# Last eight gate/up chunks on 64-row halves, two numerators moved among them, and a last tile pair that takes one tile at a time

## The chip, the cores and the metric

The kernel runs on one core of a Trainium2 chip. It is written instruction by instruction for the core's engines: TensorE (PE) for matmuls, VectorE (DVE) and ScalarE (ACT) for elementwise work and for reading PSUM, GpSimd (POOL), and SyncE (SP), whose queue starts most DMAs. PSUM, where matmuls put their results, has eight banks of 512 float32 columns in 128 partitions. The metric is device time in microseconds (us) for the whole program.

## The reference

There are 2048 tokens (x is 2048 x 640), two branches on the same x, and a gate per token that mixes them:

```python
qkv = x @ wqkv                      # 32 heads of 20
pq, pk = q @ w_phi, k @ w_phi       # per head
phi_q = concat(softmax(pq), softmax(-pq));  phi_k likewise
kv, z = sum_s phi_k * v,  sum_s phi_k
a = ((phi_q @ kv) / (phi_q @ z + 1e-6)) @ wo          # linear attention
b = (gelu(x @ w_gate) * (x @ w_up)) @ w_down          # F = 1728
g = sigmoid((x * gate_w).sum(-1))
out = g * a + (1 - g) * b
```

All inputs and the output are bfloat16.

## The kernel before, in words

Tokens are cut into 16 tiles of 128 and four blocks of four tiles. F is cut into 13 chunks of 128 columns and a tail of 64 (chunk 13). D = 640 is five pieces of 128 (`KD`). A first stage (up to some 81 us) loads x and the weights, computes q, k, v, the exponentials of the features, and sums the attention state `KV`. The change lies in what follows, `ffn`, which issues three kinds of work in a fixed order. Every engine runs its own instructions in program order; `_Sched.op` adds a semaphore wait where an instruction reads or overwrites what another engine writes or still reads (a bank of PSUM is one unit, `("ps", bank)`).

**Gate/up** (`gateup`, matmuls recorded at L464). For a block of 512 tokens and a chunk, five matmuls of 128 rows and 512 columns put x @ w_gate into one bank and five put x @ w_up into another. ScalarE writes Gelu of the first (L779), VectorE multiplies by the second into `hT` (L781). The tail chunk does gate and up in one bank; there VectorE multiplies twice (L792), one time for each half of 64 partitions, and only for every other tile, since the two halves serve tiles of different parity. Chunks take two pairs of banks in turn, (0,1) and (6,7). Each block's chunks run in the order 0, 1, 13, 2, ..., 12.

**Numerators** (`num`, `num_mms` L817, `num_steps`). For one tile, 22 matmuls of 64 rows and 66 columns (phi_q times the state, for the two signs of the softmax in alternation) fill parts of four banks, 2 to 5. VectorE then divides: eight short steps of 32 columns (L851 to L858, the first of them a reciprocal), two multiplies of 640 columns that read PSUM (`O`, L863), and one add (`Og`, L866). A DMA on SP's queue transposes Og into `goT`. The four banks come free when the second multiply at L863 has ended, since each of the two is recorded as a reader of all four. In the kernel before, tiles 0 and 1 are done together in block 1 (`num_pair`): 44 matmuls behind the fifth chunk, into six banks, with the division's steps spread over the chunks that follow, which meanwhile use other banks. The other tiles are done in the down stage.

**Down** (`down_pair`, matmuls L898). Two tiles are done together, b @ w_down and a @ wo summed in one bank for each tile and column part. All matmuls have 64 rows: the two halves of the array work at the same time, one on the first and one on the second tile, on the upper or lower 64 rows of each piece. In an opening pass each half does its rows for its tile; in a closing pass the halves change tiles. A wait on a key `("turn", bank)` keeps the two halves from writing one bank at the same time. Output columns are cut in two parts of 320, and in the last pair in parts of 256, 256 and 128, so that the last part is short. `evac` scales by the gate into `outsb` (ScalarE, and in the last pair VectorE for the second tile) and SP's queue writes the output.

A generator yields after each pair of matmuls; `downs` counts these pairs (148 in a block: 2 x (38 opening + 36 closing)) and calls `num` after certain counts. Before, these are 1, 31, 61 and 91 in blocks 0 to 2, for tiles 4b + 2 to 4b + 5, and 1 and 31 in block 3:

```python
at = (1, 31, 61, 91)
...
for b in range(self.NB):
    downs(b, {at[k]: 4 * b + 2 + k for k in range(4 if b < 3 else 2)})
```

Block 3's `hT` has no room of its own; it takes the space of x for tiles 0 to 11, which is read for the last time in block 2.

Of the kernel before, what the change touches and what calls it, by code (L numbers as in the profile page):

```python
# [3 lines left out]
P = 128  # L4
BF16 = mybir.dt.bfloat16
F32 = mybir.dt.float32
AF = mybir.ActivationFunctionType
ALU = mybir.AluOpType
# [99 lines left out]
class _Kernel:  # L108
    S, D, H, DH, F = 2048, 640, 32, 20, 1728
    KD = D // P  # L110
# [4 lines left out]
    NFC = 14  # L115
    FR = F - 13 * P
    DA = DH + 1
    DB = DH + 2
# [641 lines left out]
    def gateup(self, b, c, banks):  # L760
# [7 lines left out]
        if c < 13:  # L768
# [5 lines left out]
            for w, wk, bk in ((self.wg_sb, "wg", banks[0]), (self.wu_sb, "wu", banks[1]))[:1 if done else 2]:  # L774
                for kt in range(self.KD):
                    key = self.upheld(c)[1] if early and wk == "wu" else (wk, i, kt)
                    self.mm(bk, 0, 512, w[:, kt, c * P:(c + 1) * P], xs(kt), kt == 0, kt == self.KD - 1, xr + [key])
            up, upk = (self.upheld(c)[0], ("upf", c)) if done else (self.bank(banks[1]), ("ps", banks[1]))
            sc.op("act", lambda e: e.activation(self.gl[:, slot, :], self.bank(banks[0]), AF.Gelu_apprx_tanh),  # L779
                  reads=[("ps", banks[0])], writes=[("gl", slot)], guard=self.oldw)  # L780
            sc.op("dve", lambda e: e.tensor_tensor(hT, up, self.gl[:, slot, :], ALU.mult),  # L781
                  reads=[upk, ("gl", slot)], writes=[("hT", hk, c)], guard=old)
        else:
# [6 lines left out]
            for r in (0, 1):  # L790
                odd = lambda v: v.rearrange("p (u r q) -> p u r q", r=2, q=P)[:, :, r, :]
                sc.op("dve", lambda e: e.tensor_tensor(  # L792
                    odd(hT[64 * r:64 * r + 64, :]), odd(self.ps[64:128, bk * 512:bk * 512 + 512]),
                    odd(self.gl[64:128, slot, :]), ALU.mult),
                    reads=[("ps", bk), ("gl", slot)], writes=[("hT", hk, c, r)], guard=old)

    def before_num(self):
        return ([("upf", c) for c in self.UP + self.LATE] + ["kstage", "qstage"] + [("wref", k, h) for k in (0, 3) for h in (0, self.HM)] + [("wref", k, 0) for k in (1, 2, 4)] + [("xtok", k) for k in range(4)] + ["wkT", "wqT"])

    def num(self, t):  # L800
        NBK, DB, old = self.NUMB, self.DB, self.before_num()
        w = self.HG * DB
        base = [(NBK + 2 * s) * 512 + 512 - 6 * w for s in (0, 1)]
        self.num_mms(t, base, 0)
        rb = [("ps", NBK + k) for k in range(4)]
        for step in self.num_steps(t, base, rb, old):
            step()

    def num_mms(self, t, base, late):
        sc, w = self.sc, self.HG * self.DB  # L810
        for g in range(self.G):
            n = min(w, self.H * self.DB - w * g)
            for s in (0, 1):
                a, o = 64 * s, base[s] + w * g
                edge = o // 512 != (o + w) // 512
                first = g == 0 or (o - w) // 512 != o // 512
                sc.op("pe", lambda e: e.matmul(  # L817
                    self.ps[:, o:o + n], self.Eq[a:a + 64, g, t * P:(t + 1) * P], self.KV[a:a + 64, g, 0:n],
                    start=first and not (late and g == 0), stop=edge or g == self.G - 1, skip_group_check=True),
                    reads=[("Eq", t), "KVd", ("KV", 0), ("KV", 8), ("KV", 10)], writes=[("ps", o // 512)],  # L820
                    signal=edge or g == self.G - 1)

    def num_pair(self):
        w = self.HG * self.DB
        top = 512 - 6 * w
        over = 512 + 512 - 3 * w
        bases = [[(2 + 3 * s) * 512 + c for s in (0, 1)] for c in (top, over)]
        rb = [("ps", b) for b in range(2, 8)]
        steps = []
        for t in (0, 1):  # L830
            self.num_mms(t, bases[t], t)
        for t in (0, 1):
            n = {0: (0, 1, 3, 4), 1: (1, 2, 4, 5)}[t]
            steps.append(self.num_steps(t, bases[t], [rb[k] for k in n], self.before_num()))
        return steps

    def num_steps(self, t, base, rb, old):
# [7 lines left out]
        key = lambda k: ("RH", sl, k)  # L845
        small, wide, fin = [], [], []
        into = small

        def dve(fn, reads, writes, guard=()):
            into.append(lambda: sc.op("dve", fn, reads=reads, writes=writes, guard=guard))  # L850
        dve(lambda e: e.reciprocal(R(0), Dn[1]), rb, [key(0)], guard=old)  # L851
# [6 lines left out]
        dve(lambda e: e.tensor_tensor(R(7), R(6), R(1), ALU.mult), [key(6), key(1)], [key(7)])  # L858
        into = wide
        for s, dst in ((0, self.O1), (1, self.O2)):  # L860
# [3 lines left out]
                rb + [key(6 + s)], [("O", s, sl)], guard=old)  # L864
        into = fin
        dve(lambda e: e.tensor_tensor(self.Og[:, sl, :], self.O1[:, sl, :], self.O2[:, sl, :], ALU.add),  # L866
            [("O", 0, sl), ("O", 1, sl)], [("Og", sl)], guard=old)
        gs = t % 8
        fin.append(lambda: sc.dma("sp", lambda e: e.dma_start_transpose(self.goT[:, gs, :, :], self.Og[:, sl, :]),
                                  reads=[("Og", sl)], writes=[("goT", gs)], guard=old))  # L870

        def run(part):
            for f in part:
                f()
        return [lambda p=p: run(p) for p in (small, wide, fin)]

    def down_pair(self, t0, banks, widths):

        sc = self.sc
        ts = (t0, t0 + 1)  # L880
        NFC, KD = self.NFC - 1, self.KD
        nw = len(widths)
        hk = t0 // 4
        last = t0 + 2 == self.NT
        os_ = t0 % 4

        def mm(r, j, h, c, opens, x, n):
            t = ts[j]
            tt, gs, bk, w0, a = t % 4, t % 8, banks[h][j], sum(widths[:h]), 64 * r
            w, end = widths[h], x == n - 1  # L890
            if c <= NFC:
# [11 lines left out]
        def evac(h):  # L903
            w0, w = sum(widths[:h]), widths[h]
            for j in (0, 1):
                bk, dst, g = banks[h][j], self.outsb[:, os_ + j, w0:w0 + w], self.Gm[:, ts[j]:ts[j] + 1]
                rd, wr = [("ps", bk), "Gm"], [("outsb", os_ + j, h)]
                if last and j == 1:
                    sc.op("dve", lambda e: e.tensor_scalar(dst, self.bank(bk, w), g, None, op0=ALU.mult), reads=rd, writes=wr)
                else:  # L910
                    sc.op("act", lambda e: e.activation(dst, self.bank(bk, w), AF.Copy, scale=g), reads=rd, writes=wr)  # L911
            if last:
                hs, c0, c1 = [h], w0, w0 + w
            elif h == nw - 1:
                hs, c0, c1 = range(nw), 0, self.D
            else:
                return
            if t0 < self.TB:
                rows = self.out[0:self.BT, :].rearrange("(p j) n -> p j n", j=self.TB)[:, t0:t0 + 2, :]
            else:  # L920
                rows = self.out[t0 * P:(t0 + 2) * P, :].rearrange("(j p) n -> p j n", p=P)
            sc.dma("sp", lambda e: e.dma_start(rows[:, :, c0:c1], self.outsb[:, os_:os_ + 2, c0:c1]),
                   reads=[("outsb", os_ + j, k) for j in (0, 1) for k in hs], writes=[("out", t0, h)])

# [16 lines left out]

    NUMB = 2
    oldk = [("Ek", k, s) for k in range(5) for s in (0, 1)] + [(w, k) for w in ("Ekc", "Ekp") for k in range(5)] + [
# [5 lines left out]
    def ffn(self):  # L949
# [3 lines left out]

        def gateups(b, after, other={}):
            for idx, c in enumerate([0, 1, 13] + list(range(2, 13))):
                self.gateup(b, c, other.get(idx, pairs[self.pn % 2]))
                self.pn += 1
                after(idx)

        def downs(b, side):  # L960
            p = [pairs[(self.pn + k) % 2] for k in (0, 1)]
            n = 0
            for t in (4 * b, 4 * b + 2):
                final = t + 2 == self.NT
                for _ in self.down_pair(t, p + [(2, 3)] if final else p, (256, 256, 128) if final else (320, 320)):
                    n += 1
                    if n in side:
                        self.num(side[n])
# [7 lines left out]

        left = []

        def first_nums(idx):
            if idx == 4:  # L980
                left.extend(f for steps in self.num_pair() for f in steps)
            for _ in range({4: 1, 5: 1, 6: 2, 7: 1, 8: 1}.get(idx, 0)):
                left.pop(0)()

        def none(idx):
            pass
        at = (1, 31, 61, 91)
        gateups(0, state)
        gateups(1, first_nums, {k: ((0, 1), (0, 1), (0, 5), (1, 2))[k - 5 if k < 7 else 2 + (k - 7) % 2]
                                for k in range(5, 14)})  # L990
        gateups(2, none)
        gateups(3, none)
        for b in range(self.NB):
# [45 lines left out]
```

## Time and profile before

| | us |
|---|---|
| time, median of 3 runs | 283.51 (283.3 to 283.77) |
| span of the profiled execution, first to last instruction | 282.4 |
| gate/up matmuls of blocks 1 (from its sixth chunk) to 3, 360 in a row | 77.81 |
| numerators of tiles 0 and 1 (44 matmuls) in the chain | 0.79 |
| numerators of one tile (22 matmuls) in the down stage | 0.34 |
| 30 pairs of down matmuls between two numerators | 4.08 |
| DVE multiply `hT` (512 columns), ACT Gelu (512 columns) | 0.689, 0.597 |
| DVE multiply `O` (640 columns), reciprocal (32 columns) | 0.815, 0.357 |
| DVE multiply of the tail chunk (256 columns) | 0.427 |

The page names no time of its own for the profiled execution; its span is 1.1 us below the median of the runs, and this difference is taken as what lies around the span.

The profile is one execution on the chip. PE is the matmul engine, PEld its weight loads, which run beside the matmuls. L817 and the like are lines of the kernel before. A line of the chain gives start, length, engine, line and the number of instructions; a line of the timeline gives start, length, engine, line, operation, what is written from what, shapes, and in brackets how long the engine was idle before and who ended the wait. Where such a line holds several instructions, its length runs from the start of the first to the end of the last. A matmul's recorded duration is longer than the distance to the next one, since matmuls overlap; rates are taken from starts.

### The profile page before, as it was taken

How to read it: one execution, taken by the hardware profiler on the slowest of the kernel's cores; microseconds unless marked ns; L12 is line 12 of the kernel's file. 1: busy time of each engine (PE TensorE's matmuls, PEld its weight loads, DVE VectorE, ACT ScalarE, POOL GpSimd, SP SyncE). 2: the span in 40 equal slices, each digit the busy share in tenths (PEclk: the TensorE clock that was granted, in tenths of full speed). 3: DMA queues.
4: the chain of work that ended last, by engine and by line, in shares of the span. 5: the costliest groups of instructions: out<-in, count | busy, mean ns of one | idle time of the engine just before them, and what ended most of it. 6: DMA issues, size and time to landing. Idle time of an engine off the chain costs nothing.

```text
span 282.4 us, 6904 instructions
## 1 busy us (share of the span) xinstructions
PE 278.6 (99%) x2926; PEld 168.6 (60%) x2926; DVE 173.2 (61%) x329; ACT 105.9 (38%) x204; POOL 15.1 (5%) x69
## 2 busy tenths in 40 slices
PE   7999999999999999999999999999999999999996
PEld 4566766665665444444444444445777777777786
DVE  1456999999997523694333324235883883883801
ACT  3246978777793332223232232321112112112011
POOL 7511001101000000000000000000000000000000
PEclk9999999999999999999999999999999999999999
DMA  7999169787789910011000000000133132532221
GB/s 213 193 223 190 29 127 172 153 175 149 157 175 274 350 51 0 2 24 23 2 0 0 0 2 0 0 0 2 26 50 98 46 49 78 66 49 73 73 72 49
DMA packets 60378, 24.11 MB, mean 85 GB/s; under 512 B 51002, under 2 KB 59834, under 8 KB 60346
## 3 DMA queue, kind: packets, MB, share of 16 engines
q1 hardware_dynamic: 59680, 23.63, 38.9%
q8 instruction: 23, 0.38, 0.6%
q10 hardware_dynamic: 666, 0.03, 0.2%
q14 instruction: 9, 0.07, 0.1%
HBM read 9.04 MB, written 2.62 MB: 41 GB/s over the span
## 4 chain that ended last, share of the span: by engine, by line
PE 97%; DMA 1%; SPq 0%; ACT 0%; issue 0%
PE ps L464 58%; PE ps L898 29%; PE ps L599 4%; PE ps L817 2%; PE ps L478 2%; PE ps L637 2%; DMA w<-in_A_wqkv_dram 1%; PE ps L404 1%; SPq L230 0%; SPq L251 0%; ACT outsb L911 0%; PE ps L370 0%
## 5 line engine op out<-in xcount | busy, mean ns | idle before, releaser
L464 PE MATMUL ps<-xT,wu_sb 128*128 128x512 bf16 x260 | 64.1, 379 | 0.0
L464 PE MATMUL ps<-xT,wg_sb 128*128 128x512 bf16 x260 | 63.9, 379 | 0.0
L779 ACT ACTIVATE gl<-ps 128x512 bf16<-128x512 f32 x52 | 31.0, 597 | 70.3 <-PE ps L464 70.3
L464 PE MATMUL ps<-w,xT 128*128 128x362 bf16 (+5 forms) x340 | 51.4, 302 | 0.0
L898 PE MATMUL ps<-wd_sb,hT 64*128 64x320 bf16 x648 | 48.4, 296 | 0.0
L781 DVE TENSOR_TENSOR hT<-ps,gl 128x512 bf16<-128x512 f32 x34 | 23.4, 689 | 37.7 <-PE ps L464 37.7
L464 PEld LDWEIGHTS ps<-xT,wu_sb 128*128 128x128 bf16 x260 | 25.4, 98 | 30.3 <-DVE hT L781 0.2
L464 PEld LDWEIGHTS ps<-xT,wg_sb 128*128 128x128 bf16 x260 | 25.1, 98 | 29.8 <-issue 0.2
L911 ACT ACTIVATE outsb<-ps,Gm 128x320 bf16<-128x320 f32 (+2 forms) x31 | 14.5, 515 | 71.8 <-PE ps L898 71.8
L464 PEld LDWEIGHTS ps<-w,xT 128*128 128x128 bf16 x340 | 31.9, 97 | 14.8
L898 PEld LDWEIGHTS ps<-wd_sb,hT 64*128 64x128 bf16 x648 | 30.9, 94 | 12.2 <-issue 0.4
L898 PE MATMUL ps<-wo_sb,goT 64*128 64x320 bf16 (+2 forms) x340 | 26.5, 288 | 0.0
L617 DVE TENSOR_REDUCE Dk<-Ek 128x66 f32<-128x1320 bf16 x16 | 24.3, 1520 | 2.3 <-ACT gcol L528 2.3
L626 DVE TENSOR_TENSOR Ek<-Ek,Dk 128x1320 bf16<-128x1320 bf16 x16 | 24.5, 1532 | 0.5
L863 DVE TENSOR_TENSOR O<-ps,RH 128x640 bf16<-128x640 f32 x32 | 24.7, 815 | 0.0
L538 ACT ACTIVATE Ek<-ps 128x627 bf16<-128x627 f32 x32 | 20.5, 693 | 6.4 <-PE ps L599 4.9
L538 ACT ACTIVATE Eqt<-ps 128x627 bf16<-128x627 f32 x32 | 20.6, 705 | 2.5 <-PE ps L464 2.5
L781 DVE TENSOR_TENSOR xT<-ps,gl 128x512 bf16<-128x512 f32 x13 | 9.0, 690 | 18.2 <-PE ps L464 18.2
L898 PEld LDWEIGHTS ps<-wo_sb,goT 64*128 64x128 bf16 x340 | 15.9, 94 | 5.3
L898 PE MATMUL ps<-wd_sb,xT 64*128 64x320 bf16 (+2 forms) x270 | 16.0, 269 | 0.0
L851 DVE RECIPROCAL RH<-ps 128x32 f32<-128x32 f32 x16 | 5.7, 357 | 14.4 <-PE ps L817 14.3
L898 PEld LDWEIGHTS ps<-wd_sb,xT 64*128 64x128 bf16 x270 | 12.1, 94 | 2.7
(90 smaller groups left out, 184.1 us busy)
## 6 DMA issues: line engine op xcount, KB each, us to landing
out_dram<-outsb SPq DMA_DIRECT2D x7, 320.0 KB, 2.3
wd_sb<-in_B_w_down_dram SPq DMA_DIRECT2D x1, 2080.0 KB, 11.0
wg_sb<-in_B_w_gate_dram SPq DMA_DIRECT2D x5, 224.0 KB, 3.1
wg_sb<-in_B_w_gate_dram SPq DMA_DIRECT2D x5, 192.0 KB, 3.5
wu_sb<-in_B_w_up_dram SPq DMA_DIRECT2D x5, 192.0 KB, 3.9
wo_sb<-in_A_wo_dram SPq DMA_DIRECT2D x1, 800.0 KB, 9.7
xtok<-in_A_x_dram SPq DMA_DIRECT2D x2, 320.0 KB, 3.3
w<-in_A_wqkv_dram SPq DMA_DIRECT2D x4, 160.0 KB, 4.0
```

The costliest lines, as they stand in the source:

```text
L464: self.sc.op("pe", lambda e: e.matmul(self.ps[:, bank * 512 + c0:bank * 512 + c0 + n], lhs, rhs, start=first, stop=fin), reads=reads, writ ...
L478: sc.op("pe", lambda e, c0=c0, n=n, bk=bk, col=col: e.matmul(self.bank(bk)[:, col:col + n], self.xT[:, kt, t * P:(t + 1) * P], self.w3[:, ...
L538: self.sc.op("act", lambda e: e.activation(dst, src, AF.Exp, scale=scale), reads=[("ps", b), ("ps", b + 1)], writes=[(name, sl, s)])
L599: self.sc.op("pe", lambda e: e.matmul(out, self.xT[:, kt, t * P:(t + 1) * P], self.w3[:, kt, c:c + 2 * n].rearrange("p (r w) -> p r w", w= ...
L617: self.sc.op("dve", lambda e: e.tensor_reduce(self.Dk[:, se, 0, :].rearrange("p (u h) -> p u h", h=self.HG), self.k_view(se), AX.X, ALU.ad ...
L626: sc.op("dve", lambda e: e.tensor_tensor(v, v, R.rearrange("p (u h) -> p u h", h=self.HG).unsqueeze(3).to_broadcast([P, 2 * self.G, self.H ...
L779: sc.op("act", lambda e: e.activation(self.gl[:, slot, :], self.bank(banks[0]), AF.Gelu_apprx_tanh), reads=[("ps", banks[0])], writes=[("g ...
L781: sc.op("dve", lambda e: e.tensor_tensor(hT, up, self.gl[:, slot, :], ALU.mult), reads=[upk, ("gl", slot)], writes=[("hT", hk, c)], guard=old)
L851: dve(lambda e: e.reciprocal(R(0), Dn[1]), rb, [key(0)], guard=old)
L863: dve(lambda e, o=o, f=f, s=s: e.tensor_tensor(o, V[s][:, :, 0:DH], f, ALU.mult), rb + [key(6 + s)], [("O", s, sl)], guard=old)
L898: sc.op("pe", lambda e: e.matmul(self.bank(bk, w), lhs, rhs, start=opens and x == 0, stop=end and not opens, skip_group_check=True), reads ...
L911: sc.op("act", lambda e: e.activation(dst, self.bank(bk, w), AF.Copy, scale=g), reads=rd, writes=wr)
```

## The change

Block 3's gate/up runs apart from the others. Its first six chunks use banks 2 to 5. Then come the numerators of tile 0, in banks 0, 1, 6 and 7, and the other eight chunks, two at a time (`gateup_halves`), each pair of chunks as 20 pairs of 64-row matmuls: an opening pass in which one half of the array does gate and the other up, and a closing pass in which they change. The numerators of tile 1 come before the fifth of these eight chunks, in banks 2 to 5. `num_pair` and the special banks of block 1 are gone, and a tile's division is issued in one piece. In the down stage the numerators move to counts 12, 38, 64 and 91. In the last tile pair the three parts are no longer columns of both tiles: the first is the whole first tile (two halves of 320), the second 2 x 224 columns of the second tile, the third its last 2 x 96. For this the tail chunk of block 3 is written for all tiles in both halves of the partitions (512 instead of 256 columns for each of the two multiplies).

```diff
-                odd = lambda v: v.rearrange("p (u r q) -> p u r q", r=2, q=P)[:, :, r, :]
+                odd = lambda v: v if b == 3 else v.rearrange("p (u r q) -> p u r q", r=2, q=P)[:, :, r, :]
...
+    def gateup_halves(self, b, cs, pairs):
+        sc, KD = self.sc, self.KD
+        old = [("xT", t) for t in range(12)]
+        for close in (0, 1):
+            for c, banks in zip(cs, pairs):
+                i = 0 if c < 7 else 1
+                for kt in range(KD):
+                    for r in (0, 1):
+                        w, wk, bk = ((self.wg_sb, "wg", banks[0]), (self.wu_sb, "wu", banks[1]))[r ^ close]
+                        key = self.upheld(c)[1] if c in self.UP + self.LATE and wk == "wu" else (wk, i, kt)
+                        a, end = 64 * r, kt == KD - 1
+                        sc.op("pe", lambda e: e.matmul(
+                            self.bank(bk), w[a:a + 64, kt, c * P:(c + 1) * P],
+                            self.xT[a:a + 64, kt, b * self.BT:(b + 1) * self.BT], start=close == 0 and kt == 0,
+                            stop=close == 1 and end, skip_group_check=True),
+                            reads=[("xT", t) for t in range(4 * b, 4 * b + 4)] + [key],
+                            writes=[("ps", bk)] + ([("turn", bk)] if end else []), signal=end,
+                            after=[("turn", bk)] if close and kt == 0 else ())
+                if close:
+                    slot = self.gn % 3
+                    self.gn += 1
+                    self.gateup_evac(b, c, banks[0], slot, self.bank(banks[1]), ("ps", banks[1]), old)
...
+    def num(self, t, banks=(2, 4)):
...
+        base = [b * 512 + 512 - 6 * w for b in banks]
+        self.num_mms(t, base)
+        rb = [("ps", b + k) for b in banks for k in (0, 1)]
+        self.num_steps(t, base, rb, old)
...
-    def num_pair(self):
...
-    def down_pair(self, t0, banks, widths):
+    def down_pair(self, t0, banks, last):
...
+        if last:
+            parts = [((t0, 0, 320), (t0, 320, 320)), ((t0 + 1, 0, 224), (t0 + 1, 224, 224)),
+                     ((t0 + 1, 448, 96), (t0 + 1, 544, 96))]
+        else:
+            parts = [((t0, c, 320), (t0 + 1, c, 320)) for c in (0, 320)]
...
+                sc.dma("sp", lambda e: e.dma_start(self.out[t * P:(t + 1) * P, c0:c1], self.outsb[:, t % 4, c0:c1]),
+                       reads=[("outsb", t % 4, h, j) for j in (0, 1)], writes=[("out", t0, h)])
...
+        def last_gateups(b):
+            middle, n = [(2, 3), (4, 5)], 6
+            for idx in range(n):
+                self.gateup(b, order[idx], middle[idx % 2])
+            self.num(0, (0, 6))
+            for g, banks in enumerate((middle, pairs, pairs, middle)):
+                if g == 2:
+                    self.num(1)
+                self.gateup_halves(b, order[n + 2 * g:n + 2 * g + 2], banks)
-        at = (1, 31, 61, 91)
+        at = (12, 38, 64, 91)
         gateups(0, state)
-        gateups(1, first_nums, {k: ((0, 1), (0, 1), (0, 5), (1, 2))[k - 5 if k < 7 else 2 + (k - 7) % 2]
-                                for k in range(5, 14)})
+        gateups(1, none)
         gateups(2, none)
-        gateups(3, none)
+        last_gateups(3)
```

`gateup_evac` is the Gelu and the multiply that stood in `gateup`.

More of the change, by code (lines that the diff above doesn't have):

```diff
@@ L778, in gateup @@
             up, upk = (self.upheld(c)[0], ("upf", c)) if done else (self.bank(banks[1]), ("ps", banks[1]))
[L779 to L782, printed above, removed]
+            self.gateup_evac(b, c, banks[0], slot, up, upk, old)
         else:
@@ L795, in gateup, with gateup_evac @@
                     reads=[("ps", bk), ("gl", slot)], writes=[("hT", hk, c, r)], guard=old)
+    def gateup_evac(self, b, c, bank, slot, up, upk, old):
+        sc, hT = self.sc, self.hT(b, c)
+        sc.op("act", lambda e: e.activation(self.gl[:, slot, :], self.bank(bank), AF.Gelu_apprx_tanh),
+              reads=[("ps", bank)], writes=[("gl", slot)], guard=self.oldw)
+        sc.op("dve", lambda e: e.tensor_tensor(hT, up, self.gl[:, slot, :], ALU.mult),
+              reads=[upk, ("gl", slot)], writes=[("hT", b, c)], guard=old)
@@ L797, in before_num @@
     def before_num(self):
         return ([("upf", c) for c in self.UP + self.LATE] + ["kstage", "qstage"] + [("wref", k, h) for k in (0, 3) for h in (0, self.HM)] + [("wref", k, 0) for k in (1, 2, 4)] + [("xtok", k) for k in range(4)] + ["wkT", "wqT"])
[L800 to L807, printed above, removed]
@@ L809, in num_mms @@
-    def num_mms(self, t, base, late):
+    def num(self, t, banks=(2, 4)):
+        old = self.before_num()
+        w = self.HG * self.DB
+        base = [b * 512 + 512 - 6 * w for b in banks]
+        self.num_mms(t, base)
+        rb = [("ps", b + k) for b in banks for k in (0, 1)]
+        self.num_steps(t, base, rb, old)
+    def num_mms(self, t, base):
         sc, w = self.sc, self.HG * self.DB
@@ L818, in num_mms @@
                     self.ps[:, o:o + n], self.Eq[a:a + 64, g, t * P:(t + 1) * P], self.KV[a:a + 64, g, 0:n],
-                    start=first and not (late and g == 0), stop=edge or g == self.G - 1, skip_group_check=True),
+                    start=first, stop=edge or g == self.G - 1, skip_group_check=True),
                     reads=[("Eq", t), "KVd", ("KV", 0), ("KV", 8), ("KV", 10)], writes=[("ps", o // 512)],
                     signal=edge or g == self.G - 1)
-    def num_pair(self):
[L824 to L835, printed above, removed]
     def num_steps(self, t, base, rb, old):
@@ L845, in num_steps @@
         key = lambda k: ("RH", sl, k)
-        small, wide, fin = [], [], []
-        into = small
         def dve(fn, reads, writes, guard=()):
-            into.append(lambda: sc.op("dve", fn, reads=reads, writes=writes, guard=guard))
+            sc.op("dve", fn, reads=reads, writes=writes, guard=guard)
         dve(lambda e: e.reciprocal(R(0), Dn[1]), rb, [key(0)], guard=old)
@@ L858, in num_steps @@
         dve(lambda e: e.tensor_tensor(R(7), R(6), R(1), ALU.mult), [key(6), key(1)], [key(7)])
-        into = wide
         for s, dst in ((0, self.O1), (1, self.O2)):
@@ L864, in num_steps @@
                 rb + [key(6 + s)], [("O", s, sl)], guard=old)
-        into = fin
         dve(lambda e: e.tensor_tensor(self.Og[:, sl, :], self.O1[:, sl, :], self.O2[:, sl, :], ALU.add),
@@ L868, in num_steps @@
         gs = t % 8
[L869 to L875, printed above, removed]
-    def down_pair(self, t0, banks, widths):
+        sc.dma("sp", lambda e: e.dma_start_transpose(self.goT[:, gs, :, :], self.Og[:, sl, :]),
+               reads=[("Og", sl)], writes=[("goT", gs)], guard=old)
+    def down_pair(self, t0, banks, last):
         sc = self.sc
-        ts = (t0, t0 + 1)
-        NFC, KD = self.NFC - 1, self.KD
-        nw = len(widths)
+        NFC, KD, D = self.NFC - 1, self.KD, self.D
         hk = t0 // 4
-        last = t0 + 2 == self.NT
-        os_ = t0 % 4
+        if last:
[3 more added lines that the diff above has]
+            parts = [((t0, c, 320), (t0 + 1, c, 320)) for c in (0, 320)]
+        nw = len(parts)
         def mm(r, j, h, c, opens, x, n):
-            t = ts[j]
-            tt, gs, bk, w0, a = t % 4, t % 8, banks[h][j], sum(widths[:h]), 64 * r
-            w, end = widths[h], x == n - 1
+            t, w0, w = parts[h][j]
+            tt, gs, bk, a = t % 4, t % 8, banks[h][j], 64 * r
+            end = x == n - 1
             if c <= NFC:
@@ L903, in evac @@
         def evac(h):
-            w0, w = sum(widths[:h]), widths[h]
             for j in (0, 1):
-                bk, dst, g = banks[h][j], self.outsb[:, os_ + j, w0:w0 + w], self.Gm[:, ts[j]:ts[j] + 1]
-                rd, wr = [("ps", bk), "Gm"], [("outsb", os_ + j, h)]
+                t, w0, w = parts[h][j]
+                bk, dst, g = banks[h][j], self.outsb[:, t % 4, w0:w0 + w], self.Gm[:, t:t + 1]
+                rd, wr = [("ps", bk), "Gm"], [("outsb", t % 4, h, j)]
                 if last and j == 1:
@@ L911, in evac @@
                     sc.op("act", lambda e: e.activation(dst, self.bank(bk, w), AF.Copy, scale=g), reads=rd, writes=wr)
+            os_ = t0 % 4
             if last:
-                hs, c0, c1 = [h], w0, w0 + w
+                c1 = w0 + w
+                c0 = parts[h][0][1]
+                sc.dma("sp", lambda e: e.dma_start(self.out[t * P:(t + 1) * P, c0:c1], self.outsb[:, t % 4, c0:c1]),
+                       reads=[("outsb", t % 4, h, j) for j in (0, 1)], writes=[("out", t0, h)])
             elif h == nw - 1:
[L915 to L923, printed above, removed]
+                if t0 < self.TB:
+                    rows = self.out[0:self.BT, :].rearrange("(p j) n -> p j n", j=self.TB)[:, t0:t0 + 2, :]
+                else:
+                    rows = self.out[t0 * P:(t0 + 2) * P, :].rearrange("(j p) n -> p j n", p=P)
+                sc.dma("sp", lambda e: e.dma_start(rows[:, :, :], self.outsb[:, os_:os_ + 2, :]),
+                       reads=[("outsb", os_ + j, k, j) for j in (0, 1) for k in range(nw)], writes=[("out", t0, h)])
         wos = [NFC + 1 + k for k in range(KD)]
@@ L952, in ffn, with gateups @@
         pairs = [(0, 1), (6, 7)]
-        def gateups(b, after, other={}):
-            for idx, c in enumerate([0, 1, 13] + list(range(2, 13))):
-                self.gateup(b, c, other.get(idx, pairs[self.pn % 2]))
+        order = [0, 1, 13] + list(range(2, 13))
+        def gateups(b, after):
+            for idx, c in enumerate(order):
+                self.gateup(b, c, pairs[self.pn % 2])
                 self.pn += 1
@@ L964, in downs @@
                 final = t + 2 == self.NT
-                for _ in self.down_pair(t, p + [(2, 3)] if final else p, (256, 256, 128) if final else (320, 320)):
+                for _ in self.down_pair(t, p + [(2, 3)] if final else p, final):
                     n += 1
@@ L975, in state @@
                 self.gates()
[L977 to L983, printed above, removed]
         def none(idx):
             pass
-        at = (1, 31, 61, 91)
+        def last_gateups(b):
[8 more added lines that the diff above has]
+        at = (12, 38, 64, 91)
         gateups(0, state)
-        gateups(1, first_nums, {k: ((0, 1), (0, 1), (0, 5), (1, 2))[k - 5 if k < 7 else 2 + (k - 7) % 2]
-                                for k in range(5, 14)})
+        gateups(1, none)
         gateups(2, none)
-        gateups(3, none)
+        last_gateups(3)
         for b in range(self.NB):
```

1 line of the change is left out of this document (removed).

## The prediction

> **What bounds the kernel now.** I read the views from coarse to fine. The page first: is TensorE (PE) full, and at what clock?
>
> ```profile
> span 282.4 us, 6904 instructions
> PE 278.6 (99%) x2926; PEld 168.6 (60%) x2926; DVE 173.2 (61%) x329; ACT 105.9 (38%) x204; POOL 15.1 (5%) x69
> PEclk9999999999999999999999999999999999999999
> PE 97%; DMA 1%; SPq 0%; ACT 0%; issue 0%
> ```
>
> PE is busy 99% of the span, at full clock in every slice, and the chain that ended last is 97% PE. So a change counts only through PE: matmuls that it takes or adds, and stops that it makes. VectorE (DVE) is free 39% of the time, but this average hides where it is not. Next, the chain in order of time gives the rate of each stage:
>
> ```profile
> 116.27 0.79 PE ps L817 x44
> 117.06 77.81 PE ps L464 x360
> ...
> 195.11 0.34 PE ps L817 x22
> 195.45 4.08 PE ps L898 x60
> 199.53 0.34 PE ps L817 x22
> 199.87 4.08 PE ps L898 x60
> ...
> 230.19 7.88 PE ps L898 x116
> ```
>
> A full gate/up matmul (512 columns, 128 rows) takes 77.81/360 = 0.216 us. A pair of 64-row matmuls (320 columns) in the down stage takes 7.88/58 = 0.136, and 4.08/30 is 0.136 too: PE does not stop between the numerators. One tile's 22 numerator matmuls take 0.34. The third view is the timeline of DVE, and of PE's weight loads (PEld), around two numerators; it carries the forecast:
>
> ```profile
> 199.37 0.50 PE L817 MATMUL ps<-KV,Eq 64*128 64x66 bf16 x22
> 200.04 0.36 DVE L851 RECIPROCAL RH<-ps 128x32 f32<-128x32 f32 x1 [0.22 <-PE ps L817]
> 202.10 1.55 DVE L863 TENSOR_TENSOR O<-ps,RH 128x640 bf16<-128x640 f32 x2
> 203.74 0.49 DVE L866 TENSOR_TENSOR Og<-O,O 128x640 bf16<-128x640 bf16 x1
> 203.52 0.10 PEld L898 LDWEIGHTS ps<-wd_sb,hT 64*128 64x128 bf16 x2
> 203.70 0.37 PEld L817 LDWEIGHTS ps<-KV,Eq 64*128 64x128 bf16 x16
> ```
>
> Numerator matmuls begin at 199.37; 0.67 later DVE starts its chain; its last read of banks 2 to 5 (the second O multiply) ends at 202.10 + 1.55 = 203.65; the next tile's first weight load, into the same four banks, starts at 203.70. The first two numerators repeat this: O ends at 199.23, the load starts at 199.28, where loads otherwise go out with the pair before. So that load already waits for DVE, and the wait stays hidden under one matmul. The loop from numerator to numerator is at least 203.70 - 199.37 = 4.33 us, and 30 pairs plus 22 numerator matmuls (4.08 + 0.34 = 4.42) just cover it.
>
> **The change part by part.**
>
> *The first two numerators leave block 1.* Before them five matmuls begin at 115.03, so the next would start at 115.03 + 5 x 0.216 = 116.11; it starts at 117.00. The 44 matmuls cost 0.89, of which 2 x 0.34 is their own and 0.21 the two changes between 128-row and 64-row work. In their new place, after six chunks of block 3, all that follows is 64-row, so they cost 2 x 0.34; the one change that stood before the down stage (matmul at 194.80 instead of 193.63 + 1.08 = 194.71) now stands before them. Gain 0.21, between 0.19 and 0.23. Their two DMA transposes land some 2.6 us (the median row) after the Og add, before the down stage reads them, so they cost nothing; nothing else stands in SP's queue there, and POOL's is untouched.
>
> *The last eight chunks in row halves.* 160 matmuls of 64 rows, in 80 pairs, take the place of 80 full ones. No row has a 64-row matmul of 512 columns. Pairs take 0.136 at 320 columns and 0.031 (0.34/11) at 66, which is 0.413 ns a column and gives 0.215 at 512, against 0.216 full. I take nothing, the value of these two nearest rows. The end above, two halves that do not overlap, is 80 x 0.216 = 17.3; the 320-column pair speaks against it, so it is a rival and no term.
>
> *Waits among these chunks.* An evacuation starts 0.20 after its bank's last matmul interval (a group that ends at 193.63 is read from 193.83). Gelu takes 0.60, the multiply 0.69, a weight load follows a DVE end by 0.05. (a) The tail chunk of block 3 (13th column block, third in order) now multiplies all 512 columns per half: 0.69 (the row of that width) twice instead of 0.89 for both. In the trace its Gelu starts at 171.16 and DVE at 171.85; DVE would end at 173.27, and the chunk that takes the bank next wants it at 173.12: 0.20 to 0.29, I take 0.21. (b) Call the start of tile 0's numerators 0. The multiply of the sixth chunk ends at 0.80, DVE's chain follows to 4.4 with Og at 5.0, while PE does two chunks (20 pairs, 4.32) to 4.66: banks 0, 1, 6, 7 are free just in time, nothing. In the closing pass gate and up end together, so Gelu and multiply now follow in series: 0.20 + 0.60 + 0.05 to 0.10 + 0.69 + 0.05, about 1.6 after a chunk ends. The third group wants the second group's first banks 1.08 + 0.34 = 1.42 after that: 0.17 to 0.30, I take 0.20. (c) Tile 1's chain stands behind the second group's last multiply on DVE: it ends 0.34 + 4.9 after that group; the fourth group wants its banks after 0.34 + 0.20 + 4.32: 0.33 to 0.45, I take 0.37. Behind these chains the third group's two multiplies wait too; their banks are next used in the down stage a whole group later, so that is free. (d) Tile 2's numerators, now after 12 pairs, want banks 4 and 5 at 12 x 0.136 = 1.63 after the last chunk, whose multiply releases them after 1.6: 0 to 0.06, I take 0.01. Sum of the four: 0.79.
>
> *Numerators in the down stage at pairs 12, 38, 64, 91 instead of 1, 31, 61, 91.* The distances fall from 30 to 26, 26, 27. PE needs 26 x 0.136 + 0.34 = 3.88 for what lies between two starts, the loop through DVE 4.33. The chain's instructions and its banks are unchanged, so the cover is gone and the wait shows: everything queued on PE stands behind it. At least 4.33 - 3.88 = 0.45; at most 0.54, if the matmul trails its late weight load by 0.09, as 199.37 trails 199.28. After the drain at 194.80 both start together, which is nearest to a stopped PE, so I take 0.47, and 0.33 (0.31 to 0.40) at distance 27. Three blocks have 26, 26, 27, the last has one 26: 7 x 0.47 + 3 x 0.33 = 4.3, between 4.1 and 5.0. Og (0.49) runs on DVE while the next 22 matmuls run, so it does not lengthen the loop. The long distance, 91 to the next block's 12, is 69 pairs and takes nothing back, since PE only does its work there. The transposes of Og move with the numerators. The tightest is the second of a block, at pair 38: Og ends 4.9 after its first matmul and the transpose lands 2.6 later, 7.5 in all; its first reader, 64 pairs on, comes after 64 x 0.136 + 2 x 0.34 + 0.8 of waits = 10.2. In SP's queue the first output of a block is still issued behind it (pair 74). So the later places cost nothing there.
>
> *The last pair, one tile at a time.* 37 pairs each of 320, 224 and 96 columns instead of 256, 256 and 128. By rows: 256 takes 0.109 (275.20 to 276.62, 13 pairs), 128 takes 0.056; between them 224 is 0.096, and 96, between 66 and 128, is 0.043. 0.136 + 0.096 + 0.043 is 0.275, as before: nothing. The Trainium skill, "TensorE: Matmul & The Clock Gate", section "Wait — 56ns, not 53.3ns?", speaks against narrow pairs: matmul starts never come closer than about 25 ns. By that, two starts put a floor of 0.050 under the 96-column pair, and this part would cost 37 x 0.007 = 0.3 us, an estimate from that page. The trace decides against it, with 22 numerator matmuls in 0.34 us, two in 31 ns. At the end ScalarE reads 96 instead of 128 columns (0.473 at 256, 0.367 at 128: 0.03 less), and the final DMA moves 48 instead of 64 KB (1.6 us for 64 KB, 1.8 for 128: 0.04 less). Gain 0.07, between a gain of 0.3 (half as many pieces in that DMA, no row to price it) and a loss of 0.1.
>
> **Sum.** -0.21 + 0 + 0.79 + 4.3 + 0 - 0.07 = +4.8. The span of the profiled execution is 282.4, and the runs take 283.51, so 1.1 lies around it. With the same around it, the changed kernel has a span of 287.2 and a time of 288.3. The low ends together (-0.23 + 0.70 + 4.1 - 0.3) give 287.8, the high ends (-0.19 + 1.1 + 5.0 + 0.1) 289.5; the runs of before spread by 0.25 either way.
>
> **Rivals.**
>
> *The ten waits do not appear (not slower).* Place: the first numerator weight load of each tile in the down stage; price 4.3; it decides from a loop of 3.88 or less. For it: the list of waits has no PE idle time at the numerators. Against: loads that start 0.05 after the O multiply, twice out of two read, where they would otherwise have gone out earlier. Time 283.51 + 0.5 = 284.0.
>
> *The 64-row pairs of 512 columns are slower than one full matmul.* Each per cent on 80 pairs is 0.17; with no overlap 17.3, which gives 305.6. For it: no row of that width. Against: 0.413 ns a column in every 64-row row. A mild form (5%) gives 289.2.
>
> *A stopped PE costs more than the wait.* Weights and pair order refill, 0.1 to 0.15 more at each of 13 waits: 289.6 to 290.2. For it: the first pair after the change at 194.80 took 0.15 instead of 0.136. Against: that is 0.01.
>
> **How the numbers follow.** Forecast 0.80, waits absent 0.05, slow halves 0.07, dear restarts 0.08. Within 0.2% (0.57 us) is about what a measurement of this kernel cannot tell from no change. The forecast, the slow halves and the dear restarts are all slower: 0.95. The rival without waits is inside 0.57 but close to its edge: same 0.04, faster 0.01. The range goes from 287.4 (the low ends, less the spread of the runs) to 289.8, which takes in the mild form of both slower rivals and leaves out less than 2 in 10.
>
> **What would show it.** Right: PE idle of about 0.45 before the numerators' first weight load in the down stage, ten times, released by the O multiply, and a chain to the end that carries some 4 us of DVE; a load within 0.1 of the end of O; four gate/up waits of which the one ahead of the last two chunks is the longest; 0.216 a pair there. The forecast is wrong if numerators follow each other by 3.9 us in the down stage, or if the halves' pairs run off 0.216.

## The result, and the profile after

The changed kernel takes 288.29 us (median of 5 runs, 288.01 to 288.43) against 283.51 (5 runs, 283.23 to 283.78): 1.0172 of the time before, 95% interval 1.016 to 1.0183. The forecast was 288.3. The profiled execution has a span of 286.9 us, against 282.4; the forecast span was 287.2. The 1.1 us that were taken as lying around the span are 1.2 to 1.4 in every run whose time and span are both on record. The forecast of the time does not hang on that, since it adds 4.8 to the median before.

The page of the changed kernel, the lines that answer to those of before (engine totals, then the chain):

```profile
span 286.9 us, 7050 instructions
PE 280.4 (98%) x2994; PEld 167.8 (58%) x3006; DVE 173.8 (61%) x329; ACT 106.0 (37%) x204; POOL 15.2 (5%) x69
...
PE 5%; ACT 0%; issue 0%
PE ps L904 5%; PE ps L844 0%; ACT outsb L917 0%
```

VectorE has as many instructions as before (329) and as much work (173.8 against 173.2 us), and PE is still 98% busy: none of these totals looks like a slower kernel. What changed is how far the chain can be followed. Before, it was PE nearly from end to end; now it goes back from the end of the program only to 269.3 us, 5% of the span, and stops at a wait. The list of waits says which (who waited at which line, for whom; then us in total, times, longest):

```profile
PEld ps L844 <- DVE O L873: 5.9, 10, 0.6
PE ps L844 <- DVE O L873: 2.6, 10, 0.3
PEld ps L813 <- DVE O L873: 0.6, 1, 0.6
PEld ps L813 <- DVE xT L798: 0.5, 2, 0.3
PE ps L464 <- DVE xT L789: 0.4, 1, 0.4
```

L844 are the numerators' matmuls, L873 the multiplies `O` of their division: ten waits that the list of before did not have. Neither total is what PE loses. Where nothing waits, the numerators' first weight load starts 0.13 us before their first matmul (196.60 and 196.73 at the first numerators of block 0), so the idle time of the loads counts too much (5.9). And a matmul's recorded length, 0.30 us at 320 columns where the next pair starts 0.136 after it, covers part of the idle time of PE (2.6). The loss is read from starts. The timeline of the changed kernel at the second numerators of block 0 (start, length, engine, line, operation):

```profile
199.47 1.55 DVE L873 TENSOR_TENSOR O<-ps,RH 128x640 bf16<-128x640 f32 x2
201.10 0.49 DVE L875 TENSOR_TENSOR Og<-O,O 128x640 bf16<-128x640 bf16 x1
201.75 0.36 DVE L862 RECIPROCAL RH<-ps 128x32 f32<-128x32 f32 x1 [0.15 <-PE ps L844]
200.20 0.57 PE L904 MATMUL ps<-wo_sb,goT 64*128 64x320 bf16 x6
201.07 0.51 PE L844 MATMUL ps<-KV,Eq 64*128 64x66 bf16 x22 [0.30 <-DVE O L873]
201.07 0.40 PEld L844 LDWEIGHTS ps<-KV,Eq 64*128 64x128 bf16 x22 [0.63 <-DVE O L873]
```

The last three down pairs start at 200.20, 200.34 and 200.47, so the numerators would start at 200.61. The second O multiply ends at 199.47 + 1.55 = 201.02, the weight load follows at 201.07 and the matmul with it: 0.46 us lost. VectorE is then as before: Og runs under the matmuls, and the next reciprocal starts 0.68 after them. Over the ten places, the distance from the start of the last down matmul to that of the first numerator matmul is 0.593 to 0.600 us seven times and 0.457 to 0.460 three times. Where nothing waits it is 0.132, so 0.46 and 0.33 us are lost each time.

By stage, from starts in the profiled executions (us):

| stage | before | after | difference |
|---|---|---|---|
| start to the first Gelu of the gate/up chunks | 84.12 | 83.66 | -0.46 |
| first Gelu to the first down matmul | 110.68 | 111.44 | +0.76 |
| first to last down matmul | 85.28 | 89.61 | +4.33 |
| last matmul to the end of the span | 2.35 | 2.17 | -0.18 |

The first row holds no line of the change; over the nine profiles of this study it lies between 83.5 and 84.1. The other three rows add up to +4.9, against +4.8 in the times.

### The profile page after: what moved, and what is told of

The parts are those of the page before. It is cut to its first block, busy times and chain, and to the rows that moved or that the text cites. A ratio compares the mean times of both kernels' runs of the same rounds, so it can differ in the third digit from the quotient of the medians.

```text
span 286.9 us, 7050 instructions
## 1 busy us (share of the span) xinstructions
PE 280.4 (98%) x2994; PEld 167.8 (58%) x3006; DVE 173.8 (61%) x329; ACT 106.0 (37%) x204; POOL 15.2 (5%) x69
## 5 line engine op out<-in xcount | busy, mean ns | idle before, releaser
L464 PE MATMUL ps<-xT,wg_sb 128*128 128x512 bf16 x214 | 52.7, 379 | 0.6 <-DVE xT L789 0.4
L464 PE MATMUL ps<-xT,wu_sb 128*128 128x512 bf16 x214 | 52.9, 379 | 0.3
L464 PEld LDWEIGHTS ps<-xT,wu_sb 128*128 128x128 bf16 x220 | 21.5, 98 | 25.6
L464 PEld LDWEIGHTS ps<-xT,wg_sb 128*128 128x128 bf16 x220 | 21.1, 98 | 25.8 <-ACT gl L796 1.0
L904 PE MATMUL ps<-wo_sb,goT 64*128 64x320 bf16 (+2 forms) x340 | 25.8, 288 | 0.0
L873 DVE TENSOR_TENSOR O<-ps,RH 128x640 bf16<-128x640 f32 x32 | 24.8, 815 | 0.0
L813 PE MATMUL ps<-xT,wg_sb 64*128 64x512 bf16 x80 | 18.0, 376 | 0.1
L813 PE MATMUL ps<-xT,wu_sb 64*128 64x512 bf16 x80 | 17.5, 376 | 0.0
```

The lines of the kernel that those rows point to most:

```text
L464: self.sc.op("pe", lambda e: e.matmul(self.ps[:, bank * 512 + c0:bank * 512 + c0 + n], lhs, rhs, start=first, stop=fin), reads=reads, writ ...
L813: sc.op("pe", lambda e: e.matmul(self.bank(bk), w[a:a + 64, kt, c * P:(c + 1) * P], self.xT[a:a + 64, kt, b * self.BT:(b + 1) * self.BT], ...
L873: dve(lambda e, o=o, f=f, s=s: e.tensor_tensor(o, V[s][:, :, 0:DH], f, ALU.mult), rb + [key(6 + s)], [("O", s, sl)], guard=old)
L904: sc.op("pe", lambda e: e.matmul(self.bank(bk, w), lhs, rhs, start=opens and x == 0, stop=end and not opens, skip_group_check=True), reads ...
```

## The experiments

Each of the seven is compared with the kernel before, run beside it on the same chip; the first four ran on one chip (before: 283.46 us), the last three on another (283.30). The theory is the loop of the prediction: numerators, division on VectorE, release of banks 2 to 5, next numerators. It takes 4.35 us from start to start in the changed kernel. The rivals put the cost in the row halves, in the last pair, or on PE itself.

**Only the distances undone.** Everything of the change stays but one line.

```diff
-        at = (12, 38, 64, 91)
+        at = (12, 42, 72, 102)
```

> The changed kernel with one line altered: the numerators of the down stage at pairs 12, 42, 72 and 102, so 30 apart instead of 26, 26 and 27. Theory (the loop numerator, DVE chain, release of banks 2 to 5 takes 4.35 us, and PE has less work than that between two numerators): at 30 pairs PE has 4.42 us of work, the ten waits of 4.18 us in sum vanish, and the time is 288.3 - 4.2 = 284.1 us. Rival (the cost sits in the row halves or in the last pair, and the numerators' distance does not matter): 288.3 us.

Measured: 283.83 us (1.0012 of before, 1.0002 to 1.0022). The ten waits are gone from the list, and the down stage takes 85.29 us, as before (85.28). So the distances make the ten waits, and everything else of the change together costs 0.4 us by the times (0.1 to 0.6).

**Only the distances done.** This is the kernel before with that one line.

```diff
-        at = (1, 31, 61, 91)
+        at = (12, 38, 64, 91)
```

> The kernel before with one line altered: the numerators of the down stage at pairs 12, 38, 64 and 91, and nothing else of the change. Theory (loop of 4.35 us through DVE): seven waits of 0.46 and three of 0.32, 4.2 us in sum, 287.7 us. Rival (the cost sits in the other parts of the change): 283.5 us.

Measured: 287.62 us (1.0143, 1.0128 to 1.0158). Its list of waits has the same two totals for the numerators:

```profile
PEld ps L817 <- DVE O L863: 5.9, 10, 0.6
PE ps L817 <- DVE O L863: 2.6, 10, 0.3
```

The down stage takes 89.62 us, against 89.61 in the changed kernel. So one line of the change is the slowdown in the down stage, with or without the rest.

**A distance between.** This is the changed kernel at 28 pairs.

```diff
-        at = (12, 38, 64, 91)
+        at = (12, 40, 68, 96)
```

> The changed kernel with the numerators at pairs 12, 40, 68 and 96, 28 apart. Theory: PE has 28 x 0.136 + 0.345 = 4.15 us of work between two numerators, the loop takes 4.35, so ten waits of 0.20 remain, 2.0 us: 286.1 us. Rival one (each numerator that is not at its old place costs a fixed stop of PE): 288.3 us as the changed kernel. Rival two (distance does not matter): 288.3 us.

Measured: 286.1 us (1.009, 1.0075 to 1.0105). There are still ten waits:

```profile
PEld ps L844 <- DVE O L873: 3.6, 10, 0.4
```

By starts each is 0.19 us (0.322 to 0.326 from the last down matmul, less 0.132), and the down stage takes 87.30. The numerators' distance from start to start is 4.35, as at 26 pairs: PE's work between them grew by two pairs, and the loop did not move. A fixed stop per moved numerator is excluded, as is a time that does not depend on the distance: either would have left 288.3.

**The loop made shorter, the distances left.** The two multiplies do half of their columns.

```diff
-            o = dst[:, sl, :].rearrange("p (h d) -> p h d", d=DH)
-            f = R(6 + s).unsqueeze(2).to_broadcast([P, H, DH])
-            dve(lambda e, o=o, f=f, s=s: e.tensor_tensor(o, V[s][:, :, 0:DH], f, ALU.mult),
+            HN = 16
+            o = dst[:, sl, 0:HN * DH].rearrange("p (h d) -> p h d", d=DH)
+            f = R(6 + s)[:, 0:HN].unsqueeze(2).to_broadcast([P, HN, DH])
+            dve(lambda e, o=o, f=f, s=s: e.tensor_tensor(o, V[s][:, 0:HN, 0:DH], f, ALU.mult),
```

(O is set to zero once before, on GpSimd.)

> The changed kernel, its numerators at 12, 38, 64 and 91 as they are, but the two O multiplies do 16 of the 32 heads (320 instead of 640 columns); the other heads' output is left zero, so half of the attention branch is left out. Each multiply should take about 0.49 instead of 0.815 us, and the loop 4.35 - 0.65 = 3.70 us, below the 3.88 us of PE work at distance 26. Theory: all ten waits vanish without any matmul moved, and so does most of the wait before the last two chunks: 283.8 us. Rival (what costs is on PE itself: the interruption, the order of the pairs, the weight loads): 288.3 us.

Measured: 283.49 us (1.0003, 0.9994 to 1.0013). The timeline of VectorE in the down stage:

```profile
199.12 0.88 DVE L874 TENSOR_TENSOR O<-ps,RH 128x320 bf16<-128x320 f32 x2
200.09 0.49 DVE L876 TENSOR_TENSOR Og<-O,O 128x640 bf16<-128x640 bf16 x1
200.93 0.36 DVE L862 RECIPROCAL RH<-ps 128x32 f32<-128x32 f32 x1 [0.35 <-PE ps L844]
204.80 0.36 DVE L862 RECIPROCAL RH<-ps 128x32 f32<-128x32 f32 x1 [0.34 <-PE ps L844]
```

The pair of multiplies takes 0.88 instead of 1.55, VectorE now waits 0.35 for PE, and the reciprocals follow each other at 204.80 - 200.93 = 3.87 us: the 3.88 of PE's work. No numerator waits, with 26 pairs between them and the same matmuls as in the changed kernel. So the wait is the loop's length against PE's work, and its release is the end of O. The wait before the last two chunks went too (0.27 us), and the stage before the down stage takes 110.95 instead of 111.44. Not all of that is a gain: the two halves of the array, which fall one matmul apart in this stage (see (b) further down), here stay so to the end, and the down stage takes 85.49 us, 0.21 more than before.

**The last pair alone.** This is the kernel before with the new parts of the last pair, and what they need; a part of the edit is shown.

```diff
-                odd = lambda v: v.rearrange("p (u r q) -> p u r q", r=2, q=P)[:, :, r, :]
+                odd = lambda v: v if b == 3 else v.rearrange("p (u r q) -> p u r q", r=2, q=P)[:, :, r, :]
...
+            parts = [((t0, 0, 320), (t0, 320, 320)), ((t0 + 1, 0, 224), (t0 + 1, 224, 224)),
+                     ((t0 + 1, 448, 96), (t0 + 1, 544, 96))]
```

> The kernel before with the last pair alone changed: one tile at a time (320, 224 and 96 columns) and, for that, the tail chunk of block 3 multiplied for all 512 columns in both halves. Theory: the two wider multiplies hold the tail chunk's bank 0.30 us longer than its next user can wait (as the trace of the changed kernel has it), and the short end saves 0.07: 283.7 us. Rival (the last pair by itself is faster by its half-sized final transfer, 0.3 us or more): 283.4 us or less. Both are near what the measurement can tell, so the trace's wait behind the tail chunk counts.

Measured: 283.95 us (1.0025, 1.0016 to 1.0034). The trace has one new wait, 0.30 us behind the tail chunk of block 3, the down stage at 85.29 (85.28 before), and 0.05 less after the last matmul: +0.25 by the trace, +0.65 by the times. The wait is shown, and the rival (283.4 or less) is out. The other 0.4 us are in no stage of the profiled executions: the span is 282.5 in one and 282.4 in the other, while the medians of all spans are 282.6 and 282.1. The profile of before shows one of its longer executions, with the longest first stage of all (84.12). Where the 0.4 us lie stays open. In the changed kernel the wait is this (the tail chunk's two multiplies, and the next user of its bank):

```profile
170.62 1.42 DVE L789 TENSOR_TENSOR xT<-ps,gl 64x512 bf16<-64x512 f32 x2 [1.08 <-ACT gl L784]
172.15 0.77 PEld L464 LDWEIGHTS ps<-xT,wg_sb 128*128 128x128 bf16 x5 [0.60 <-ACT gl L796]
172.18 1.24 PE L464 MATMUL ps<-xT,wg_sb 128*128 128x512 bf16 x5 [0.35 <-DVE xT L789]
```

The multiplies end at 172.04; the chunk that wants the bank had its turn at 171.88. (The view puts the wait of the load down to a Gelu, but that Gelu ended at 171.60; the multiply ended last.)

**Two waits of the gate/up stage taken away.** The distances are 30 as above, the first six chunks of block 3 take three bank pairs, and VectorE's list of instructions is shifted by two.

```diff
-        sc.op("dve", lambda e: e.reciprocal(self.Gr[:, :], self.gcol[:, :]), reads=rd, writes=["Gr"])
+        for _ in range(3):
+            sc.op("dve", lambda e: e.reciprocal(self.Gr[:, :], self.gcol[:, :]), reads=rd, writes=["Gr"])
...
-                self.gateup(b, order[idx], middle[idx % 2])
+                self.gateup(b, order[idx], (2, 3) if idx in (0, 3, 5) else (4, 5) if idx in (1, 4) else (0, 1))
...
-            for g, banks in enumerate((middle, pairs, pairs, middle)):
+            for g, banks in enumerate((middle[::-1], pairs, pairs, middle)):
```

> The changed kernel with numerators at 12, 42, 72 and 102, and two edits more: block 3's first six chunks take three bank pairs so that the tail chunk's bank is not wanted again for three chunks, and VectorE repeats one reciprocal of 16 columns twice, early, so that every later VectorE instruction is two places further on. Theory: the 0.30 us wait behind the tail chunk of block 3 vanishes; and the 0.4 us stop of VectorE, which in six profiles stood at the same place (191) of its instruction list, stays at that place and so falls on an earlier chunk with slack, which takes away the 0.12 us wait behind the tail chunk of block 2. 283.8 - 0.30 - 0.12 = 283.4 us. Rival for the stop (it belongs to the tail chunk of block 2 and its work): it stays on that chunk, and the wait of 0.12 us with it.

Measured: 283.4 us (1.0006, 0.9996 to 1.0015), so 0.1 above the kernel before, where the run with the distances alone was 0.4 above its own. The two intervals overlap; the trace decides. In it both waits are gone, and the stage before the down stage takes 111.02 instead of 111.44, which is 0.42 less, as forecast. The tail chunk of block 2 on VectorE, first in the changed kernel, then in this one:

```profile
141.72 0.89 DVE L789 TENSOR_TENSOR hT<-ps,gl 64x256 bf16<-64x256 f32 x2 [1.44 <-PE ps L464]
```

```profile
141.28 0.89 DVE L790 TENSOR_TENSOR hT<-ps,gl 64x256 bf16<-64x256 f32 x2 [1.08 <-ACT gl L785]
```

VectorE was idle 1.44 us there and is 1.08 here, as at the tail chunks of blocks 1 and 3; the chunk that takes the bank next no longer waits 0.12 us. So the stop did not belong to that chunk.

**Row halves undone.** This is the last run with the eight chunks on full rows.

```diff
-                self.gateup_halves(b, order[n + 2 * g:n + 2 * g + 2], banks)
+                for j in (0, 1):
+                    self.gateup(b, order[n + 2 * g + j], banks[j])
```

> As the run with the three bank pairs and the shifted VectorE list, but the last eight chunks on full rows, in the same banks and with the numerators in the same places: the row halves alone are undone. Theory: two numerators among full-row chunks cost 0.21 each for the changes of row grouping, where the halves have none (+0.42 less the 0.09 that the halves pay before the numerators and full rows pay before the down stage, so no difference there), but gate ends 1.08 us before up again, and the two waits of 0.54 us among the last eight chunks vanish: -0.1 us, 283.3 us. Rival (64-row pairs of 512 columns are themselves slower or faster than full matmuls): the difference comes out otherwise, and the chunks' rate in the trace differs from 0.216 us.

Measured: 283.83 us (1.0013, 1.0003 to 1.0023), where 283.3 was expected. By the trace the stage before the down stage is 0.14 shorter than with the halves (110.88 against 111.02), as expected: PE pays five changes of row grouping instead of one (0.09 to 0.10 each) but has no wait among these chunks. By the times the run is 0.4 longer; in the profiled execution 0.34 us more pass after the last matmul, where the final transfer of the same 48 KB took 1.8 us instead of 1.5. The two intervals overlap, so the times do not decide what the halves are worth; in the trace they gain nothing.

No variant that does all of the work beats the kernel before: the best one is at 1.0006, within what can be measured.

## Why the prediction was right, point by point

*What bounds the kernel* held: the time moved by what PE lost, with VectorE's share unchanged at 61%. The 61% is an average; in the down stage VectorE's chain and PE's work between two numerators were level before (4.42 against a loop of 4.33 to 4.35), and the change took four pairs (at one place in three, three) from one side.

*The numerators in the down stage*: 4.3 forecast (4.1 to 5.0), 4.33 measured, by a stage comparison that the run with this one line repeats to 0.01. By starts a wait is 0.46 and 0.33 us, where 0.47 and 0.33 were forecast, 4.2 in all; the 22 matmuls behind a wait take 0.01 longer (0.357 instead of 0.347), which makes up the rest. The choice to let the matmul start with its late weight load, as after the change at 194.80, was right: both start at 201.07.

*The first two numerators*: a gain of 0.21 was forecast. The changes of row grouping cost 0.10, 0.09 and 0.10 before and 0.10 now, which is a gain of 0.19.

*Row halves at the rate of full rows* was right. In the changed kernel pairs of 64 x 512 start 0.215 to 0.216 us apart (186.62, 186.84, 187.05). The 17.3 us of that rival are nowhere.

*The waits of the gate/up stage*: 0.79 forecast, and 0.30 + 0.54 + 0.12 = 0.96 measured, which with the gain above gives the +0.76 of the stage. (a) The tail chunk of block 3: 0.21 taken, at most 0.29; it was 0.30, since the weight load came 0.11 after the multiply's end and not 0.05, and the matmul 0.03 behind it. (b) and (c), 0.20 and 0.37, lose 0.54 together, of 0.57 forecast, but not in the way that was forecast. The timeline of the changed kernel at the third group, and where the fourth begins:

```profile
185.92 0.37 PE L813 MATMUL ps<-xT,wg_sb 64*128 64x512 bf16 x1
186.17 0.09 PEld L813 LDWEIGHTS ps<-xT,wu_sb 64*128 64x128 bf16 x1 [0.18 <-DVE xT L798]
...
190.77 0.09 PEld L813 LDWEIGHTS ps<-xT,wg_sb 64*128 64x128 bf16 x1 [0.60 <-DVE O L873]
```

At (b) only the up bank was still held. The half that wanted it started at 186.18, 0.25 late (0.17 to 0.30 forecast). The gate's half went ahead alone, and from then on it ran one matmul ahead of the other half; the prediction took both halves to wait. The pairs were full again, only shifted, so the loss shows only at the end of the group, as one unpaired matmul (190.29). Then (c), released by the second O multiply of tile 1, holds the last two chunks 0.27 longer. (d) 0.01 was forecast, and none was seen. The 0.12 behind the tail chunk of block 2 was not forecast at all. So the longest single wait of this stage was the one behind the tail chunk (0.30), and the one ahead of the last two chunks, which was to be the longest, is that only together with the unpaired matmul.

*The last pair*: no change of the matmuls was forecast, and with the last pair alone the down stage differs by 0.01. The narrow pairs kept pace: pairs of 96 columns start 0.042 apart (284.67 and 284.71 in the changed kernel), and the two matmuls of a pair 3 ns apart. So the floor of 25 ns between matmul starts, which the Trainium skill states ("TensorE: Matmul & The Clock Gate", "Wait — 56ns, not 53.3ns?"), does not bound a pair on two row halves here: 0.050 in place of 0.042 in each of 37 pairs would have shown as 0.3. The end took 0.18 less where 0.07 was forecast, but over the variants with this end it ran from 0.20 less to 0.17 more, so what it gains cannot be told from these profiles.

*The rivals.* The one without waits at the numerators is refuted by the ten waits. The dear restart of a stopped PE comes to 0.01, not 0.1 to 0.15. Of what was to show the steps, the chain to the end was a wrong pointer: it did not carry VectorE's 4 us, it ended at the last wait. The list of waits and the starts did show it.

*The sum* came out at 288.3 as forecast, and to that digit by luck. By the stages of the profiles the waits of gate/up are 0.17 above their term and the end 0.11 below, with 0.03 and 0.02 from the other two; the times then moved 0.1 less than these stages. What was not luck is the term of the numerators, nine tenths of the sum, which four runs confirm.

## What to carry to other kernels

Where an engine feeds another and gets its buffers back, compare the loop's length with the work in between in that stage, and look whether a first load already starts right behind the release: then the spacing is at its limit though no wait shows. Beyond what slack there is (here 4.42 less 4.35, 0.07 us), a few units less in between cost their full length, each time. And giving two streams a common end (here gate and up) delays the release of the second: Gelu and multiply now follow in series, and the up bank comes free 1.6 us after its chunk's last matmul interval (184.50 to 186.12 in the changed kernel) instead of 0.9 (194.71 to 195.60 before). That costs as soon as the bank is wanted within that time.

## What the runs showed of the hardware that was not expected

VectorE stood still for 0.4 us at a fixed place of its instruction list. In the kernel before and in six others the entry with index 191 of its recorded instructions (counted from 0, waits included) starts 0.40 to 0.41 us after the end of the entry ahead of it, at two different places of the program: a gate/up multiply at 124.92 in the kernel before, where VectorE had time to spare, the tail chunk of block 2 at 141.72 in the changed kernel, where PE then waited 0.12. A transfer on one of the two instruction queues starts 0.70 and 0.67 us later in these two. With two instructions more ahead of it, the tail chunk ran on time. Entry 191 is then an earlier multiply, at 139.51, that waits for its matmuls in any case, so a stop there would not show; but the transfer moved with it and starts 0.66 us later (140.17). That it is the supply of instructions is an inference from the place and the queue, not shown.
